# Strassen's scheme for 20 of the 28 F blocks of a GEGLU down projection, its sums made in place in shared memory

## The chip, the cores and the metric

The kernel runs on one core of a Trainium2 chip. The time is the device time of one execution in microseconds, median of several runs. The runs of the kernel before lie within 0.3% of each other. One early run of the kernel before took 1173.4 us, more than double the others. Being over 1.5% above the fastest it counts as slow and is left out. The traces show five engines that matter here: TensorE (PE, matmuls; PEld is its weight load), VectorE (DVE), ScalarE (ACT), GpSimd (POOL) and SyncE (SP), which issues most of the DMAs (108 of the 111 in the change's trace).

## The reference

```python
B, S, D, F = 1, 2048, 1024, 3584          # all bfloat16
def reference(x, w_gate, w_up, w_down):
    return (gelu_tanh(x @ w_gate) * (x @ w_up)) @ w_down
```

## The kernel before

The 2048 tokens are worked in two halves of 1024. Each half first makes h (gate and up, product with gelu) and keeps it in `hT`, 28 blocks of 128 F rows; then it computes down for two groups of 512 tokens. Gate and up already use Strassen's scheme (in Winograd's form): two F blocks and two halves of D make a 2 x 2 block product, which takes seven products and not eight. Its sums of weights (s1 to s4, on POOL) and of x (t1 to t4, on DVE, t4 on POOL) are fp32r tiles (fp32r is a 32-bit float type, printed as f32 in the rows of matmuls; one of 512 columns took 0.2286 us here, a bf16 one 0.2159); the plain blocks a22 and b22 are cast to fp32r by ACT. One `pair_quads` call makes two F blocks of gate and of up in 56 matmuls:

```python
for j in range(2):                                  # gate, up
    mm(PB[j], j, block(key, j, 0, 0), b11, True)    # m1, bf16
    act(nc.scalar.copy(out=banks[QB[j]][:], in_=banks[PB[j]][:]))
for j in range(2):
    mm(VB[j], j, s(j, "s1"), tsum["t1"], True)      # m5, fp32r
    ...
    prep(j, "s1")                                   # s1 of the next pair
# ... m6 = s2 t2 on QB, m2 on PB, m7 = s3 t3 on RB, m3 = s4 b22 on QB, m4 = a22 t4 on RB
```

Down is plain: per group 28 blocks x 8 banks of bf16 matmuls, `wd` streamed in tiles of two blocks, all eight of the kernel's `banks` in use.

```python
for kk, b in step:
    ts, dn = grp * TSB + b // 2, b % 2
    for c in range(WDT):
        nc.tensor.matmul(banks[b][:], lhsT=hT[:, kk * WDT + c, ts * P : (ts + 1) * P],
                         rhs=wd_tiles[base + kk][:, c, c0 : c0 + DN], ...)
```

In the down stage DVE, ACT and POOL have next to nothing to do but read the banks out and prepare the next half.

## Time and profile before

| | before |
|---|---|
| time, median of the fast runs | 562.3 us (562.25 to 562.6) |
| span of the profiled run | 560.4 us |
| PE busy | 552.3 us, 99% |
| one group of down (224 bf16 matmuls) | 48.35 us |
| one gate/up pair (16 bf16, 40 fp32r matmuls) | 12.60 us |
| granted clock of PE | 1.000 |

PE hardly waits in the two stages (0.9 us in front of all of down's matmuls, 1.4 in front of those of the pairs): the starts of its matmuls are evenly spaced (0.2159 us in down), so the time is the number of matmuls by their pace. The lines for that are in the prediction. Four more groups of the kernel before give the durations of what the change uses more of (line, engine, operation, out<-in, shapes, count | busy us, mean ns | idle before):

```profile
L340 PEld LDWEIGHTS bank<-t,s 128*128 128x128 f32 x624 | 117.4, 188 | 28.9
L444 PEld LDWEIGHTS <-hT 128*128 128x128 bf16 x896 | 87.5, 98 | 105.8 <-issue 0.5
L205 POOL TENSOR_TENSOR t<-xT,t 128x2048 fp32r<-128x2048 bf16 x2 | 8.2, 4081 | 0.0
L200 DVE TENSOR_TENSOR t<-xT,t 128x2048 fp32r<-128x2048 bf16 x2 | 4.6, 2287 | 9.7 <-DMA xT<-in_x_dram 9.7
```

The last two lines are how the change's sums look when nothing holds them up: DVE needs 2.3 us for 2048 columns, POOL 4.1.

### The profile page before, as it was taken

What the parts mean: (1) busy time and instruction counts of PE and PEld (TensorE: products, weight loads), DVE (VectorE), ACT (ScalarE), POOL (GpSimd) and SP (SyncE); (2) the same over time, 40 slices, a digit from 0 to 9 for tenths busy, and PEclk for the clock granted to TensorE, in tenths of its full rate; (3) what the DMA queues carried; (4) which work ended last, traced back from release to release, by engine and by line L of the source; (5) the groups of instructions that cost most, each with busy time, mean ns of one, the idle gap of its engine ahead of it and who ended that gap; (6) DMA issues with size and microseconds to landing.
All of it is one profiled execution on the core that took longest, in us unless ns stands there. A gap on an engine that the chain in (4) does not pass through costs nothing.

```text
span 560.4 us, 6719 instructions
## 1 busy us (share of the span) xinstructions
PE 552.3 (99%) x2475; PEld 334.9 (60%) x2521; DVE 175.7 (31%) x241; ACT 200.2 (36%) x342; POOL 248.2 (44%) x216
## 2 busy tenths in 40 slices
PE   8999999999999999999999999999999999999997
PEld 4457777667767544444467667767777664444443
DVE  1724444443344200113044443344444440001001
ACT  2435455555555100102055555555555540001001
POOL 0587777766774000003547766777777700000000
PEclk9999999999999999999999999999999999999999
DMA  9540412406100267987723140404070004446443
GB/s 274 176 149 2 150 61 91 131 20 205 58 2 1 60 192 226 254 236 240 256 77 95 56 150 2 150 1 150 22 241 3 0 1 135 158 155 230 151 150 112
DMA packets 61008, 67.54 MB, mean 121 GB/s; under 512 B 14768, under 2 KB 44720, under 8 KB 60976
## 3 DMA queue, kind: packets, MB, share of 16 engines
q1 hardware_dynamic: 60288, 66.46, 37.5%
q10 hardware_dynamic: 688, 0.66, 0.4%
q8 instruction: 20, 0.33, 0.2%
q14 instruction: 12, 0.10, 0.1%
HBM read 59.77 MB, written 4.19 MB: 114 GB/s over the span
## 4 chain that ended last, share of the span: by engine, by line
PE 98%; DMA 1%; issue 0%; ACT 0%; ACTq 0%
PE bank L340 58%; PE bank L444 34%; PE bank L211 5%; DMA wu_sb<-in_w_up_dram 1%; PE bank L265 0%; ACT o_sb L458 0%; ACTq L135 0%; ACTq L458 0%
## 5 line engine op out<-in xcount | busy, mean ns | idle before, releaser
L444 PE MATMUL bank<-wd_sb,hT 128*128 128x512 bf16 x878 | 192.8, 379 | 0.9
L340 PE MATMUL bank<-t,s 128*128 128x512 f32 x624 | 160.9, 406 | 0.0
L444 PEld LDWEIGHTS <-hT 128*128 128x128 bf16 x896 | 87.5, 98 | 105.8 <-issue 0.5
L316 POOL TENSOR_TENSOR s<-wg_sb 128x512 fp32r<-128x512 bf16 x52 | 62.2, 1196 | 198.8 <-DMA wg_sb<-in_w_gate_dram 105.3
L340 PEld LDWEIGHTS bank<-t,s 128*128 128x128 f32 x624 | 117.4, 188 | 28.9
L358 DVE TENSOR_TENSOR bank<-bank,m 128x512 f32<-128x512 f32 x104 | 72.6, 699 | 124.0 <-ACT bank L377 112.3
L226 DVE TENSOR_TENSOR hT<-g_sb,bank 128x512 bf16<-128x512 f32 x112 | 76.9, 688 | 68.0 <-ACT g_sb L221 31.1
L221 ACT ACTIVATE g_sb<-bank 128x512 f32<-128x512 f32 x112 | 66.6, 597 | 87.4 <-DVE bank L358 49.9
L458 ACT CAST o_sb<-bank 128x512 bf16<-128x512 f32 x16 | 9.4, 586 | 157.6 <-PE bank L444 140.3
L316 POOL TENSOR_TENSOR s<-wu_sb 128x512 fp32r<-128x512 bf16 x52 | 62.4, 1200 | 0.1
L460 DVE CAST o_sb<-bank 128x512 bf16<-128x512 f32 x16 | 11.1, 691 | 159.6 <-PE bank L444 136.4
L340 PE MATMUL bank<-xT,wg_sb 128*128 128x512 bf16 x183 | 52.5, 382 | 1.3
L340 PE MATMUL bank<-xT,wu_sb 128*128 128x512 bf16 x208 | 53.4, 379 | 0.1
L340 PE MATMUL bank<-b,s 128*128 128x512 f32 x208 | 51.4, 389 | 0.0
L340 PE MATMUL bank<-t,a 128*128 128x512 f32 x208 | 51.4, 389 | 0.0
L340 PEld LDWEIGHTS bank<-b,s 128*128 128x128 f32 x208 | 39.0, 188 | 8.2
L340 PEld LDWEIGHTS bank<-t,a 128*128 128x128 f32 x208 | 39.0, 188 | 8.1
L373 ACT COPY m<-bank 128x512 f32<-128x512 f32 x52 | 30.6, 588 | 17.7 <-PE bank L340 17.7
L377 ACT COPY bank<-bank 128x512 f32<-128x512 f32 x52 | 29.6, 570 | 17.0 <-PE bank L340 17.0
L329 ACT CAST a<-wg_sb 128x512 fp32r<-128x512 bf16 x26 | 16.2, 621 | 54.0 <-PE bank L340 29.2
L340 PEld LDWEIGHTS <-wu_sb 128*128 128x128 bf16 x208 | 20.3, 98 | 24.7 <-issue 0.3
L369 ACT COPY bank<-bank 128x512 f32<-128x512 f32 x52 | 29.6, 570 | 14.4 <-PE bank L340 13.6
(28 smaller groups left out, 238.2 us busy)
## 6 DMA issues: line engine op xcount, KB each, us to landing
wd_sb<-in_w_down_dram SPq DMA_DIRECT2D x56, 512.0 KB, 3.5
wg_sb<-in_w_gate_dram SPq DMA_DIRECT2D x11, 1024.0 KB, 5.4
wu_sb<-in_w_up_dram SPq DMA_DIRECT2D x11, 1024.0 KB, 7.5
out_dram<-o_sb SPq DMA_DIRECT2D x15, 256.0 KB, 2.7
wg_sb<-in_w_gate_dram SPq DMA_DIRECT2D x11, 256.0 KB, 4.0
wu_sb<-in_w_up_dram SPq DMA_DIRECT2D x11, 256.0 KB, 4.1
xs<-in_x_dram SPq DMA_DIRECT2D x2, 512.0 KB, 5.7
xT<-in_x_dram SPq DMA_TRANSPOSE x17, 3.8
```

The lines of the kernel that those rows point to most:

```text
L211: return nc.tensor.matmul(ps[:], lhsT=w_sb[:, kd, fi * P : (fi + 1) * P], rhs=xT[:, kd, tb * TB : (tb + 1) * TB], start=(kd == 0), stop=(k ...
L221: act(nc.scalar.activation(out=g_sb[:], in_=ps[:], func=ACT.Gelu_apprx_tanh))
L226: nc.vector.tensor_tensor(out=hT[:, fc, tb * TB : (tb + 1) * TB], in0=g_sb[:], in1=ps[:], op=ALU.mult,)
L316: pool(nc.gpsimd.tensor_tensor(out=t[:], in0=in0, in1=in1, op=op))
L329: act(nc.scalar.copy(out=t[:], in_=a(1, 1)))
L340: nc.tensor.matmul(banks[bank][:], lhsT=lhs[:, c, :], rhs=rhs[:, c, :], start=start and c == 0, stop=c == KH - 1, skip_group_check=True,)
L358: nc.vector.tensor_tensor(out=banks[dst][:], in0=banks[src][:], in1=m5[j][:], op=ALU.add)
L369: act(nc.scalar.copy(out=banks[QB[j]][:], in_=banks[PB[j]][:]))
L373: act(nc.scalar.copy(out=m5[j][:], in_=banks[VB[j]][:]))
L377: act(nc.scalar.copy(out=banks[RB[j]][:], in_=banks[QB[j]][:]))
L444: nc.tensor.matmul(banks[b][:], lhsT=hT[:, kk * WDT + c, ts * P : (ts + 1) * P], rhs=wd_tiles[base + kk][:, c, c0 : c0 + DN], start=(kk == ...
L460: dve(nc.vector.tensor_copy(out=dst, in_=banks[b][:]))
```

## The change

In down, the first 20 F blocks (as 2 x 10) against the two halves of D, and the first 256 against the last 256 tokens of a group, become a 2 x 2 block product by Strassen; the last 8 F blocks stay plain and add to the same banks. A group then needs 204 matmuls, of which 100 are fp32r, in place of 224 bf16 ones. The new sums get no memory of their own: they live in the memory of gate and up's sums (`t_mem`, `s_mem`), and the rows of `wd` in that of gate and up's weights (`w_mem`). Each sum overwrites the one before it: t2 replaces t1 block by block as m5 is done with it, t4 replaces t2, b22 replaces t3, and so for s. They are made anew for each of the four groups. The core of the diff:

```diff
+    t_mem = shared_pool.tile([P, 5 * KH * TB], F32R, name="t_mem")
+    s_mem = shared_pool.tile([P, 10 * KH * P], F32R, name="s_mem")
+    w_mem = shared_pool.tile([P, 4 * KD * FG + 4 * KD * P], BF16, name="w_mem")
 ...
+        product("m1", PB, h_block(0, 0), wd_block(0, 0), True)
+        # copy PB to QB (ACT)
+        product("m5", VB, lsum(0), rsum(0), True, behind=to_s2_t2)   # t2[i] DVE, s2[i] POOL
+        # copy VB to m5 (ACT)
+        product("m6", QB, lsum(0), rsum(0),
+            behind=lambda i: s_down(hT, grp, "s4", i, i + 1))        # POOL
+        for u in range(2):
+            act(nc.scalar.copy(out=banks[RB[u]][:], in_=banks[QB[u]][:]))
+            add_m5(QB[u], QB[u], u)                                  # DVE
+        for i in range(NS):
+            t_down("t4", i, i + 1)                                   # DVE
+        product("m2", PB, h_block(0, 1), wd_block(1, 0))
+        product("m7", RB, lsum(1), rsum(1), behind=lambda i: t_down("b22", i, i + 1))
+        for u in range(2):
+            add_m5(VB[u], RB[u], u)                                  # DVE: VB = RB + m5
+        # a22 (ACT)
+        product("m3", QB, lsum(0), rsum(1))
+        product("m4", RB, lsum(1), rsum(0))
+        # then 64 plain matmuls for the last 8 blocks, and the read-out
 ...
+        then0 = {                                # first group of a half
+            "m5": next_t("t3", 5),               # t3 of this group, DVE
+            "m4": next_t("t3", 5) + next_t("t1", 5) + [next_group],
+        }                                        # next_group: s1, s3 of the second group, POOL
```

(Cuts: comments in place of the copies, the loads, the sums' bodies and the last pair's `then`, in which s1, s3 and t1 of the first group are made.)

## The prediction

> **What bounds the kernel now.** I read the page's busy shares and slices, then the chain that ended last, then the timeline of TensorE (PE).
>
> ```profile
> PE 552.3 (99%) x2475; PEld 334.9 (60%) x2521; DVE 175.7 (31%) x241; ACT 200.2 (36%) x342; POOL 248.2 (44%) x216
> ...
> PEclk9999999999999999999999999999999999999999
> ...
> PE 98%; DMA 1%; issue 0%; ACT 0%; ACTq 0%
> PE bank L340 58%; PE bank L444 34%; PE bank L211 5%; DMA wu_sb<-in_w_up_dram 1%; PE bank L265 0%; ACT o_sb L458 0%; ACTq L135 0%; ACTq L458 0%
> ```
>
> PE is busy throughout at full clock, and is 98% of the chain; 34% is L444, the down matmuls. Busy is not pace, so I take paces from starts in PE's timeline:
>
> ```profile
> 161.79 1.04 PE L340 MATMUL bank<-xT,wg_sb 128*128 128x512 bf16 x3
> ...
> 174.39 1.04 PE L340 MATMUL bank<-xT,wg_sb 128*128 128x512 bf16 x3
> ...
> 186.99 96.87 PE L444 MATMUL bank<-wd_sb,hT 128*128 128x512 bf16 x439
> 283.69 0.81 PE L340 MATMUL bank<-xT,wg_sb 128*128 128x512 bf16 x3
> ```
>
> The down stage of one half is 283.69 - 186.99 = 96.70 us for 448 matmuls in the code (records are missing, x439): 0.2159 us each, 48.35 us per group of 224. A Strassen pair is 174.39 - 161.79 = 12.60 us for 16 bf16 and 40 fp32r matmuls, so an fp32r one costs (12.60 - 16 x 0.2159) / 40 = 0.2286 us. Only PE's work counts today. The other engines matter for what the change gives them, and one pair of rows warns about that, the first sums, where VectorE (DVE) and GpSimd (POOL) run together (timeline, 19.9 to 26.5 us):
>
> ```profile
> 20.02 2.28 DVE L200 TENSOR_TENSOR t<-xT,t 128x2048 fp32r<-128x2048 bf16 x1
> ...
> 20.64 2.68 POOL L316 TENSOR_TENSOR s<-wg_sb 128x512 fp32r<-128x512 bf16 x1 [19.33 <-DMA wg_sb<-in_w_gate_dram]
> ...
> 22.82 2.65 DVE L202 TENSOR_TENSOR t<-xT 128x2048 fp32r<-128x2048 bf16 x1
> ...
> 23.43 3.05 POOL L316 TENSOR_TENSOR s<-wu_sb 128x512 fp32r<-128x512 bf16 x1
> ...
> 26.44 1.15 POOL L316 TENSOR_TENSOR s<-s,wg_sb 128x512 fp32r<-128x512 f32 x1
> ```
>
> Alone, the POOL op takes 1.15 us. Here each ends about 1.01 us after the DVE sum beside it (22.30 to 23.32, 25.47 to 26.48), and the second DVE sum, 0.36 us longer than the first, ends 2.15 us after POOL's (23.32 to 25.47). They took turns.
>
> [...]a DVE op with one PSUM input doesn't stretch POOL (1.15 to 1.19 us within the pairs)[...]. [...]188 ns per fp32 load, 98 per bf16 load; at 0.2286 us per matmul the load is mostly hidden. [...]
>
> **Part by part, PE.** Per group, 20 F blocks go from 160 bf16 matmuls to 140: m1 and m2, 40 bf16; m5, m6, m7, m3, m4, 100 fp32r. The 8 plain blocks stay 64. New group: 104 x 0.2159 + 100 x 0.2286 = 22.45 + 22.86 = 45.31 us. That saves 3.04 us per group, 12.2 us over four groups: 562.3 - 12.2 = 550.1, 2.2% faster, if nothing waits.
>
> **Sums.** Each group needs t1 to t4 on DVE, 10 x 512 columns each, both inputs in SBUF; s1 to s4 on POOL, 10 x 256 columns each; b22 and a22 on ACT (about 10 x 0.62 and 5 x 0.62 us, behind m7 and m3, with some 2 us to spare). Taking turns, I estimate 0.55 us for 512 columns on DVE (2.15 / 4, rounded up) and 0.52 us for 256 on POOL (1.01 / 2, rounded up): a turn of both is 1.07 us. Alone they repeat every 0.60 and 0.63 us. All eight sums are 4 x 5.5 + 4 x 5.2 = 43 us of the shared way in per group, against 45 us of PE work. So it hardly has slack, and each sum has a deadline.
>
> **Second group of a half.** T is us from its m1. PE alone: m1 to 4.3, m5 to 8.9, m6 to 13.5, m2 to 17.8, m7 to 22.4, m3 to 26.9, m4 to 31.5, plain to 45.3. t2 and s2 are made in place, block by block, behind m5's reads, from T = 5.0; ten turns end at 15.7. m6 wants block 9 at 13.0; it ends at 16.3, so 2.8 us of wait. Then s4 has POOL nearly alone, t4 is done by about 27 and m4 may start at 29.7 as PE gets there. The group takes 45.3 + 2.8 = 48.1 us, 0.25 less than before.
>
> **First group of a half.** It starts behind, and has t3 to make as well. In the last gate/up pair t1 and the 1024-column pieces of s1 and s3 (2.0 us each) take turns, and DVE's order places t1 after the pair's adds; I get the last piece of t1 at T = 9.6, where m5's block 8 wants it at 8.0 (wait 1.6). POOL has done s2[0], s2[1]; eight turns to 18.2, two more t2 (with s4[0..1]) to 20.3; m6 ends at 20.8, 7.3 late in all. DVE then has, in order, t3 (5.4 us, three s4 between: 27.3), two adds of m5 (1.4: 28.7), three turns of t4 with s4 (31.9), seven t4 alone (36.1), and only then the adds of m5 to VB from RB (36.8, 37.5). m4 writes RB, so its second matmul waits to 37.5; PE would be there at about 34.5. m4 ends at 41.9, the plain blocks at 55.7. That is 7.3 us more than the old 48.35. Sums for the second group run in the plain part: t3, t1, s1 end near 53.5, s3 later; the next m5 is at 60, no wait.
>
> **Sum.** Two halves: 2 x (7.3 - 0.25) = 14.1 us more: about 576 us. As my turns may be pessimistic, and such a schedule was probably laid out with care, I put the point a little lower, at 574.
>
> **DMA.** wd falls from 56 loads of 0.5 MB to 16 plus 2 x 5 MB. The risk is the second group of the first half: two new weight chunks (2 MB each) and one wd tile stand ahead of the next wd tile in SP's queue. At 0.35 to 0.38 MB/us, as the DMA rate at 83 to 86 us shows, 4.7 MB from T = 27 land by about 42, the tile by 43.5, and PE wants it at about 45. Close, but I count nothing.
>
> **Rivals.** (1) Everything hides: 550 us. For it: PE never waits now, and the sums are cut so finely that PE could follow them. Against: the two stretched POOL rows. If only m6's short wait were left in each group, 4 x 2.8 gives 561. (2) The sums take turns as above and m6 and the first groups' m4 wait: 570 to 581; for it, the rows shown. (3) fp32r is slower here, as weights change bank at every matmul: each 0.01 us on 400 matmuls is 4 us; against, 40 in a row at 0.2286 now. (4) The wd tile late behind the chunks: 1 to 4 us, once. (5) PE's clock drops in the waits; the trace shows 0.9 or more in every slice, but has no such waits. It would add several us.
>
> **Range and chances.** 574 us, range 560 to 584: the low end is m6's wait alone, the high end rival 2 plus a few us of 3, 4 or 5. Faster by over 2% needs under 551.1, so no wait above 1 us in total: 0.06. Slower by over 2% needs over 573.6, near the middle of rival 2: 0.52. Within 2%: 0.42.
>
> **What would show it.** In the changed profile: first groups of about 55 us and second ones of about 48; PE waiting on POOL and DVE sums in m6 and on a DVE add at m4; POOL's 256-column sums stretched from about 0.65 to over 1 us and DVE's from 0.69 to over 1 where both run, and not where one runs alone; fp32r pace near 0.2286 where PE doesn't wait. The prediction is wrong if the small sums overlap unstretched, if a first group is under 50 us, or if the lost time is in front of a DMA.

The sum is 562.3 + 2 x (7.3 - 0.25) = 576.4 us, from which the point was set at 574. Its "0.60 and 0.63 us" are estimates that can be worked out from the trace of the kernel before: DVE starts its next operation 0.60 us after a 512-column one (22.22 to 22.82), and POOL's 512-column sums start 1.12 us apart (26.44 to 27.56), less 256 columns at 1.90 ns, (4081 - 1155) / 1536, for 0.63.

## The result, and the profile after

The change takes 590.7 us (590.0 to 590.9, 4 runs) against 562.3 us for the kernel before, ratio 1.050 (95% interval 1.048 to 1.052): slower. Ratios here are the mean time of one kernel's fast runs over that of the other's of the same rounds, so not quite the ratio of the medians that I quote.

The page after, for the lines shown of before:

```profile
PE 556.5 (95%) x2400; PEld 364.3 (62%) x2441; DVE 334.8 (57%) x365; ACT 244.5 (42%) x426; POOL 409.6 (70%) x328
PE   8999999999999795999999999999999997599897
DVE  0724443344446999778544434444434499994841
PEclk9999999999999997999999999999999999979999
PE 86%; DVE 8%; issue 3%; POOL 1%; DMA 1%; ACT 0%; DVEq 0%; POOLq 0%
```

PE's row has two dents (a 7 and a 5 close together, in each half's down stage), just where DVE's row goes to 9; the clock's row has a 7 at the 5 of the first half and next to that of the second; and DVE is now 8% of the chain that ended last. PE's busy time hardly moved though it has 75 records fewer: the dents cost what the matmuls saved, and more.

PE's timeline in the first half's down stage (start us, us, instructions, and the idle time before them with its releaser) shows the steps; the first group runs from 188.12 to 250.01:

```profile
188.12 4.49 PE L533 MATMUL bank<-w_mem,hT 128*128 128x512 bf16 x19
...
195.76 1.21 PE L533 MATMUL bank<-t_mem,s_mem 128*128 128x512 f32 x4 [0.39 <-DVE t_mem L491]
...
207.18 0.70 PE L533 MATMUL bank<-t_mem,s_mem 128*128 128x512 f32 x2 [0.38 <-DVE t_mem L491]
209.03 4.26 PE L533 MATMUL bank<-w_mem,hT 128*128 128x512 bf16 x19
212.94 9.44 PE L533 MATMUL bank<-t_mem,s_mem 128*128 128x512 f32 x40
228.85 7.49 PE L533 MATMUL bank<-t_mem,s_mem 128*128 128x512 f32 x20 [6.47 <-DVE bank L573]
236.18 13.99 PE L533 MATMUL bank<-wd_sb,hT 128*128 128x512 bf16 x62
250.01 4.48 PE L533 MATMUL bank<-w_mem,hT 128*128 128x512 bf16 x20
...
298.36 1.89 PE L361 MATMUL bank<-xT,w_mem 128*128 128x512 bf16 x8
```

The rows read as m1; m5 in pieces; m6 in pairs of matmuls every 1.08 us; m2; m7 and m3; then a gap of 6.47 us; m4, which takes 236.18 - 228.85 = 7.33 us where m7 and m3 took about 4.6 each; and the plain blocks. The group is 61.89 us long, against 48.35 before. The second group runs from 250.01 to 298.36, 48.35 us. The second half repeats it: 61.94 us for its first group. So the loss is 2 x 13.6 = 27.1 us in the first groups, and nothing in the second ones. The remaining 1.1 us of the profiled run is in its first 12 us, where PE was slow for longer: its first 16 small matmuls of x take 1.89 us and in the profile before 1.07 (the recorded clock is 1.00 in both, so it doesn't show why). In the profiles of e1 to e7, whose PE work is the same up to there, the first group starts at 186.95 to 188.61 us, so I don't charge this to the change.

What DVE and POOL did meanwhile, from their timelines:

```profile
193.23 11.09 POOL L510 TENSOR_TENSOR s_mem<-s_mem,hT 128x256 fp32r<-128x256 f32 x10 [0.86 <-PE bank L533]
204.28 14.24 POOL L510 TENSOR_TENSOR s_mem<-hT,s_mem 128x256 fp32r<-128x256 bf16 x10
218.90 7.43 POOL L510 TENSOR_TENSOR s_mem<-hT 128x512 fp32r<-128x512 bf16 x5 [0.38 <-PE bank L533]
...
197.24 10.87 DVE L491 TENSOR_TENSOR t_mem<-w_mem,t_mem 128x512 fp32r<-128x512 bf16 x10
208.03 7.05 DVE L491 TENSOR_TENSOR t_mem<-w_mem 128x1024 fp32r<-128x1024 bf16 x3
215.00 1.28 DVE L573 TENSOR_TENSOR bank<-bank,m 128x512 f32<-128x512 f32 x2
216.20 11.89 DVE L491 TENSOR_TENSOR t_mem<-w_mem,t_mem 128x512 fp32r<-128x512 bf16 x10
228.01 1.28 DVE L573 TENSOR_TENSOR bank<-bank,m 128x512 f32<-128x512 f32 x2
```

POOL's three rows are s2, s4 and the next group's s1; DVE's are t2, t3, the adds to QB, t4 and the adds to VB. t2 takes 1.08 us a block beside s2. t4 takes 11.89 us, about 1.6 us a block in the stretch beside s1, although t4 and s1 share no data. DVE is busy without a break from 197 to 229 us, and the last thing in its queue is what m4 waits for: m4 writes RB, and the adds to VB read RB.

The clock, by stretches (window, its length, busy us and count of PE, PEld, DVE, ACT, POOL; then PE's granted clock, DMA share, GB/s):

```profile
222.40:228.85 6.45, 0.00 (x1) 0.03 (x1) 6.45 (x7) 0.00 (x0) 3.94 (x3) 0.91 0.00 0
228.85:232.00 3.15, 3.15 (x7) 2.40 (x8) 3.15 (x3) 0.00 (x0) 0.85 (x1) 0.50 0.00 0
232.00:236.20 4.20, 4.20 (x15) 3.11 (x14) 4.20 (x3) 0.00 (x0) 4.20 (x2) 0.71 0.00 0
```

During the gap the granted clock fell to half (0.50 from 227.64 to 234.48 us, worked out from windows of 1 us), and m4 then ran through 5.6 us of it.

### The profile page after: what moved, and what is told of

It is laid out like the page before. It is cut to its first block, busy times and chain, and to the rows that moved or that the text cites. A ratio compares the mean times of both kernels' runs of the same rounds, so it can differ in the third digit from the quotient of the medians.

```text
span 588.5 us, 7109 instructions
## 1 busy us (share of the span) xinstructions
PE 556.5 (95%) x2400; PEld 364.3 (62%) x2441; DVE 334.8 (57%) x365; ACT 244.5 (42%) x426; POOL 409.6 (70%) x328
## 4 chain that ended last, share of the span: by engine, by line
PE 86%; DVE 8%; issue 3%; POOL 1%; DMA 1%; ACT 0%; DVEq 0%; POOLq 0%
PE bank L361 54%; PE bank L533 27%; DVE t_mem L491 8%; PE bank L229 5%; POOL s_mem L510 1%; DMA w_mem<-in_x_dram 1%; PE bank L283 0%; DVE hT L244 0%; DVE bank L384 0%; DVE bank L573 0%; ACT o_sb L643 0%; DVEq L491 0%; DVEq L244 0%; POOLq L510 0%
## 5 line engine op out<-in xcount | busy, mean ns | idle before, releaser
L361 PE MATMUL bank<-t_mem,s_mem 128*128 128x512 f32 x1040 | 255.2, 399 | 0.0
L361 PEld LDWEIGHTS bank<-t_mem,s_mem 128*128 128x128 f32 x1040 | 195.4, 188 | 45.3
L335 POOL TENSOR_TENSOR s_mem<-w_mem 128x512 fp32r<-128x512 bf16 x104 | 121.6, 1190 | 111.1 <-PE bank L361 81.2
L533 PE MATMUL bank<-t_mem,s_mem 128*128 128x512 f32 x400 | 108.5, 418 | 24.9 <-DVE bank L573 12.9
L533 PEld LDWEIGHTS bank<-t_mem,s_mem 128*128 128x128 f32 x400 | 75.9, 197 | 55.2 <-POOL s_mem L510 22.0
L361 PE MATMUL bank<-xT,w_mem 128*128 128x512 bf16 x392 | 97.7, 380 | 1.3
L491 DVE TENSOR_TENSOR t_mem<-w_mem,t_mem 128x512 fp32r<-128x512 bf16 x80 | 84.3, 1123 | 8.2 <-PE bank L533 8.2
L510 POOL TENSOR_TENSOR s_mem<-hT 128x512 fp32r<-128x512 bf16 (+1 forms) x32 | 67.7, 2142 | 18.8 <-PE bank L533 10.4
L491 DVE TENSOR_TENSOR t_mem<-w_mem 128x1024 fp32r<-128x1024 bf16 (+2 forms) x28 | 64.5, 2352 | 0.0
L335 POOL TENSOR_TENSOR s_mem<-s_mem,w_mem 128x512 fp32r<-128x512 f32 x52 | 63.3, 1240 | 0.0
L335 POOL TENSOR_TENSOR s_mem<-w_mem,s_mem 128x512 fp32r<-128x512 bf16 x52 | 60.0, 1175 | 0.0
L533 PE MATMUL bank<-wd_sb,hT 128*128 128x512 bf16 x248 | 55.4, 379 | 0.4
```

The costliest lines, as they stand in the source:

```text
L335: pool(nc.gpsimd.tensor_tensor(out=t, in0=in0, in1=in1, op=op))
L361: nc.tensor.matmul(banks[bank][:], lhsT=lhs[:, c, :], rhs=rhs[:, c, :], start=start and c == 0, stop=c == KH - 1, skip_group_check=True,)
L491: dve(nc.vector.tensor_tensor(out=t, in0=in0, in1=in1, op=ALU.subtract))
L510: pool(nc.gpsimd.tensor_tensor(out=t, in0=in0, in1=in1, op=op))
L533: nc.tensor.matmul(banks[bank][:], lhsT=lhs, rhs=rhs, start=start, stop=stop, skip_group_check=True,)
```

## The experiments

The theory after reading the trace: (a) a DVE sum with two SBUF inputs and a POOL sum exclude each other; (b) in the first groups that makes DVE's queue the bound, with s1 of the next group in it as an uninvited guest, as nothing in its data holds it behind t4; (c) m4 hangs on DVE's order, not on its own data; (d) the gap costs a second time, through the clock. The rivals: the small sums are slow by themselves; fp32r matmuls are slower in down; m4 is slow because of its operands. Each run below is beside the kernel before on the same chip (medians 563.6, 562.2 and 562.4 us for the three sets). "First" and "second" are the groups of a half; two numbers are those of both halves. The group times are those of the profiled run, which for e5_split is its slowest (589.65 us, where the fastest took 586.45).

| run | time us | ratio (95%) | first groups us | second group us, first half |
|---|---|---|---|---|
| before | 562.3 | 1 | 48.35 | 48.35 |
| the change | 590.7 | 1.050 (1.048 to 1.052) | 61.9, 61.9 | 48.4 |
| e3_write (wrong result) | 551.2 | one look | 45.3, 45.3 | 45.2 |
| e1_hold | 576.7 | 1.023 (1.021 to 1.026) | 56.3, 54.7 | 48.4 |
| e2_fill | 587.1 | 1.042 (1.040 to 1.044) | 59.5, 61.1 | 48.3 |
| e4_add | 585.9 | 1.040 (1.038 to 1.041) | 59.2, 60.0 | 49.5 |
| e5_split | 587.6 | 1.045 (1.042 to 1.048) | 62.1, 62.2 | 48.0 |
| e6_holdadd | 573.7 | 1.020 (1.018 to 1.021) | 52.5, 52.5 | 50.9 |
| e7_dve24 | 570.2 | 1.013 (1.011 to 1.015) | 53.2, 53.2 | 46.9 |
| e8_dve | 571.5 | 1.018 (1.014 to 1.021) | 49.1, 49.1 | 55.3 |
| e10_chunk | 558.2 | 0.993 (0.991 to 0.994) | 49.1, 49.1 | 45.4 |
| e11_s3 | 557.3 | 0.991 (0.989 to 0.992) | 48.0, 48.0 | 45.6 |

All but e3_write gave the reference's result.

### Do the sums exclude each other? (e3_write)

```diff
-        pool(nc.gpsimd.tensor_tensor(out=t, in0=in0, in1=in1, op=op))
+        for _ in range(2):
+            pool(nc.gpsimd.memset(t.bitcast(F32), 0.5))
```

> Wrong result on purpose: every down sum on GpSimd becomes two memsets of the same block, which write SBUF and read nothing. Theory, the clash is at the reads of SBUF: DVE's 512-column sums fall from 1.08 and 1.65 us apart to 0.60 even where GpSimd is busy, m6 and m4 don't wait, groups of 45.3 to 46, time about 550 to 553. Rival, any work on GpSimd slows DVE, or DVE is slow in place: DVE's spacing stays above 0.8 us where GpSimd is busy and m6 still waits.

DVE's and POOL's timelines, first group:

```profile
193.19 6.11 DVE L491 TENSOR_TENSOR t_mem<-w_mem,t_mem 128x512 fp32r<-128x512 bf16 x10
205.96 6.10 DVE L491 TENSOR_TENSOR t_mem<-w_mem,t_mem 128x512 fp32r<-128x512 bf16 x10
...
193.21 12.53 POOL L511 MEMSET s_mem<- 128x256 f32 x40 [2.75 <-PE bank L534]
```

POOL is busy without a break beside t2 (40 memsets in 12.53 us), but it no longer reads SBUF, and t2 takes 6.11 us for ten blocks and not 10.87. That clears the small sums on DVE and leaves the exclusion at the reads. The time of this single run was 551.2 us and the groups 45.25 us: the prediction's 45.31 us of PE work for a group, so fp32r is not slower in down either. This is what the change is worth when its sums are free.

### The guest in the queue (e1_hold)

```diff
+        def hold_pool():      # one column of t4's last block: waits for t4
+            pool(nc.gpsimd.tensor_copy(out=hold_sb[:],
+                in_=right(0, NS - 1, NS)[:, 0, DN - 1 :].bitcast(F32)))
-            "m4": next_t("t3", 5) + next_t("t1", 5) + [next_group],
+            "m4": [hold_pool] + next_t("t3", 5) + next_t("t1", 5) + [next_group],
```

> The next group's s1 sums are held on GpSimd until t4 is done (a one-column copy that reads t4's last block). Theory, DVE and GpSimd take turns at SBUF and s1 ran ahead into t4: t4 drops from 11.9 to about 7.5 us, PE's wait before m4 from 6.45 to about 2 us, m4 then stays at full clock (4.6 us and not 7.3), each first group falls from 61.9 to about 55, the time to about 577. Rival, DVE's small sums are slow by themselves: t4 stays near 11.9 us, time 590. Second groups stay at 48.35 in both.

t4 in the first half, PE's m4 in both, and the clock in the first half:

```profile
216.70 7.06 DVE L491 TENSOR_TENSOR t_mem<-w_mem,t_mem 128x512 fp32r<-128x512 bf16 x10
...
224.52 6.72 PE L534 MATMUL bank<-t_mem,s_mem 128*128 128x512 f32 x20 [1.62 <-DVE bank L574]
505.57 5.11 PE L534 MATMUL bank<-t_mem,s_mem 128*128 128x512 f32 x20 [1.65 <-DVE bank L574]
...
226.00:228.00 2.00, 2.00 (x6) 1.59 (x5) 2.00 (x2) 0.00 (x0) 2.00 (x2) 0.50 0.00 0
```

t4 took 7.06 us as expected and the gap 1.62 us: 14.0 us of the time came back. That shows theory (b). One thing was not as expected: the clock halved here too, after a much shorter gap. In the second half the gap was as long (1.65 us), the clock stayed at 1.00 and m4 took 4.96 us; the two first groups differ by that, 56.3 and 54.7 us. The four runs show the same two outcomes: two have a mean granted clock of 0.997 (578.3 and 578.0 us), two of 1.000 (575.3 us both).

### Is it the gap that makes m4 slow? (e2_fill)

```diff
+        if grp == 0:
+            for i in range(20):                      # adds zero to m2's banks
+                mm(PB[i % 2], zero_sb[:], b_block(0, 0, 0, 1)[:, 0, :])
         product("m4", RB, lsum(1), rsum(0))
```

> 20 matmuls by a zero weight, added to m2's bank, fill 4.3 us of PE's wait before m4 in the first groups. Theory, m4 ran at half clock because PE sat idle for 6.45 us: the granted clock stays 1.0 in m4, it takes 4.5 to 4.7 and not 7.3 us, time about 585 (2 x 2.8 less). Rival, m4 is slow because its operands or banks come late, one by one: m4 stays 7.3 us, time 590 to 591.

In the first half m4 took 4.95 us at clock 1.00, in the second half 6.55 us with the clock at half for part of it, though the rest of the gap was the same in both (2.13 and 2.12 us). The time fell by 3.6 us of the 5.7 expected. So the theory holds where the clock held, m4's operands are cleared, and after a gap of 2 us the clock can go either way. A fill that leaves less of a gap was not tried.

### Does m4 need t4 or DVE's order? (e4_add, then e6_holdadd)

```diff
-        for i in range(NS):
+        for i in range(5):
             t_down("t4", i, i + 1)
 ...
             add_m5(VB[u], RB[u], u)
+        for i in range(5, NS):
+            t_down("t4", i, i + 1)
```

> The two adds of m5 to VB from RB move ahead of the last five t4 blocks in DVE's order. Theory, m4 waits for all of t4 only by DVE's order (it writes RB, which those adds read): m4 starts right behind m3 and then follows t4 block by block, ending some 4 us earlier in each first group, clock at full or nearly, time about 582. Rival, m4 waits for the t4 data itself: its last block sets the end either way, at best 1 to 2 us less per group, time 587 or more. In second groups nothing changes.

m4 did start right behind m3 (0.60 us of gap), so the wait was one of order. But t4's last five blocks still took turns with s1 at about 1.6 us each, PE followed them two matmuls at a time, and the clock halved in that sparse stretch (no gap over 0.92 us, PE busy 55% and 35% of the two 2 us windows from 226 to 230 us; 0.50 from 231.2 to 233). The gain was 4.8 us and not 9: the rival was nearer on the size, as the order and s1 cover for each other. The second group of the first half, 49.5 us, waited 1.00 us for a late `wd` tile; more on that below. Both edits together tell that:

> Both earlier edits of the first groups: s1 of the next group held until t4 is done, and the adds of m5 to VB ahead of t4's last five blocks. Theory, these were two separate causes of one wait, and the half clock its sequel: first groups fall from 56.3 (hold alone) to about 53, m4 at 4.6 us and full clock, time about 570. Rival, the hold took the whole wait already and the rest is in m5 and m6: time 574 to 577.

The first groups fell to 52.5 us, under the 53 expected, and the clock stayed up (1.00 in both groups of the first half). The time did not reach 570, as the second group of the first half lost 2.5 us: its m6 waited longer, as s3, now later, ran on into it (the hold's one-column copy itself took 8.32 us here, beside DVE's sums of t3 and t1, and 0.18 in e1_hold), and a `wd` tile came 1.52 us late. This is the transfer that the prediction had called close: two weight chunks for the next half stand ahead of it in SP's queue. What made it late is the edit itself: the `w_up` part of the first chunk goes where t4 reads rows of `wd`, t4's last blocks now come after m7's adds, and SP sends the first piece of `w_up` 28.8 us after the group's start and not 25.6 as in the change (28.0 in e4_add). e1_hold, with shorter first groups but t4 in its old place, sends it at 25.6 and has no late tile.

### Is m6's wait the sums' pace? (e5_split)

The first half of m2 moves ahead of m6:

```diff
+        product("m2", PB, h_block(0, 1), wd_block(1, 0), i1=5)
         product("m6", ...)
 ...
-        product("m2", PB, h_block(0, 1), wd_block(1, 0))
+        product("m2", PB, h_block(0, 1), wd_block(1, 0), i0=5)
```

> The first half of m2 (10 bf16 matmuls, 2.16 us, no sums needed) moves between m5 and m6. Theory, PE waits in m6 for ten turns of t2 and s2, and in the first groups m4's start is set by DVE's queue, not by PE: second groups fall from 48.35 to about 46.2 us, first groups stay at 61 to 62, time about 586.5. Rival, fp32r matmuls are slower in the down stage and the loss lies there: second groups stay near 48.3, time 590.

The second group went to 48.0 us, of which 0.93 us was the late `wd` tile: 47.1 us where 46.2 was expected and 48.35 was the rival. m6 ended 16.6 us after the group's start, as in the change (16.8), though 2.16 us of other work had been put ahead of it: PE's work was hidden in the wait, and t2 and s2 set its end. The first groups stayed at 62 us, as expected. So fp32r's pace is out as a cause, but most of this move's gain was taken back at once by the tile and by small waits behind it; alone it is worth 0.5% at best.

### Sums that exclude each other, on the faster engine (e7_dve24, e8_dve)

```diff
-        pool(nc.gpsimd.tensor_tensor(out=t, in0=in0, in1=in1, op=op))
+        if name in DVE_S or (name, grp) in DVE_S:
+            dve(nc.vector.tensor_tensor(out=t, in0=in0, in1=in1, op=op))
+        else:
+            pool(nc.gpsimd.tensor_tensor(out=t, in0=in0, in1=in1, op=op))
+    DVE_S = ("s2", "s4")        # e7; its hold, as in e1_hold, is cut here
```

> With the hold, s2 and s4 are made on DVE, not on GpSimd (0.33 us for 256 columns by 1.04 ns a column, where GpSimd takes 0.52 in its turn). Theory, sums that exclude each other cost least on the faster engine: t2 and s2 together 0.93 us a block and not 1.08, second groups about 46.9, first ones about 52.5, time about 566. Rival, two engines still overlap in part and one engine with more work is slower: m6 ends later than now, time above 577.

```profile
241.45 4.48 PE L539 MATMUL bank<-w_mem,hT 128*128 128x512 bf16 x20
256.76 4.26 PE L539 MATMUL bank<-w_mem,hT 128*128 128x512 bf16 x19
...
288.31 1.89 PE L361 MATMUL bank<-xT,w_mem 128*128 128x512 bf16 x8
```

The second group is 288.31 - 241.45 = 46.86 us, the 46.9 expected: a block of t2 and s2 now takes 0.94 us on one engine, and took 1.08 us on two; on DVE a 256-column sum gives way to the next operation after 0.33 us (196.98 to 197.31). The 1.04 ns a column is an estimate from the kernel before, (2287 - 688) / 1536 for DVE's operations of 2048 and 512 columns. The first groups are 53.2 us (52.5 expected), the time 570.2 (566 expected). The rival is out.

e8_dve goes on: all down sums on DVE but the first s1, t1 earlier in the last pair, m2 split, the adds to QB ahead of s4, the adds to VB ahead of t4.

> All of it: every down sum on DVE but the first s1 (GpSimd, in the last pair, while DVE reads PSUM), t1 started earlier in that pair, m2 split around m6, adds to QB ahead of s4 and to VB ahead of t4. Theory, the change's arithmetic is worth having once the sums don't exclude each other: second groups 45.3 to 45.6 us (no wait), first groups 48 to 50, time about 559, just under the kernel before. Rival, the sums are too many for DVE's order in the first groups: these stay above 52, time above 565.

The first groups came to 49.1 us in both halves, as expected. The second ones did not, for two new waits that the trace names:

```profile
239.94 5.95 PE L538 MATMUL bank<-w_mem,hT 128*128 128x512 bf16 x19 [2.92 <-DVE o_sb L655]
286.80 5.30 PE L538 MATMUL bank<-wd_sb,hT 128*128 128x512 bf16 x15 [3.46 <-DMA wd_sb<-in_w_down_dram]
...
521.07 4.26 PE L538 MATMUL bank<-w_mem,hT 128*128 128x512 bf16 x19 [2.92 <-DVE o_sb L655]
```

m1 of the second group waited for DVE to read the banks out behind the sums in its queue, and the `wd` tile came 3.46 us late (t4 is last in DVE's order here, and SP's first piece of `w_up` went out 32.6 us after the group's start). Both gaps of the first half brought the half clock with them (0.53 on average from 240 to 243 us, 0.83 from 286 to 289): m1 took 5.95 us for what takes 4.3. In the second half a gap as long, 2.92 us, did not slow it: m1 took 4.26 us.

### A version that is faster than both (e10_chunk, e11_s3)

Both start from e8_dve. The cut shows what e10_chunk adds to it (the call of the new `done("end")` is left out); e11_s3 also makes 4 blocks of the first groups' s3 on POOL.

```diff
-                on_act = b % 2 == (1 if last_grp else 0)
+                on_act = grp == 0 or b % 2 == (1 if last_grp else 0)
 ...
-                lambda: w_fill(1),                  # after the group's first plain step
+            then1["end"] = [lambda: w_fill(1)]      # after its last wd tile
```

> The version of before with every down sum on DVE, and its two leftovers mended: the first groups' banks are read out by ACT alone (m1 of the second group had waited 2.92 us for DVE's read-out behind the sums), and the second weight chunk of the next half is loaded after the group's last wd tile (a tile had come 3.46 us late behind it). Theory: these waits and the half clocks after them go, first groups 49, second 45.3 to 46, time 558 to 560, just faster than the kernel before (ratio 0.992 to 0.996). Rival, ACT's read-outs or the chunk then come late: time above 563.

> As the run beside it, and 4 of the 10 blocks of the first groups' s3 are made on GpSimd in the last pair, where DVE mostly reads PSUM. Theory: 1.1 us less in DVE's queue ahead of t3, so m7 waits about 1 us less in each first group, 48 us each, time about 557. Rival, GpSimd's pieces hold up t1 on DVE and m5 waits instead: no gain, 559 or more.

Both came in as expected, 558.2 and 557.3 us. e11_s3 is 0.9% faster than the kernel before (ratio 0.991, 0.989 to 0.992): clear of the noise. Its page and PE's timeline:

```profile
PE 547.1 (98%) x2400; PEld 360.9 (65%) x2441; DVE 319.9 (58%) x463; ACT 247.7 (45%) x434; POOL 265.2 (48%) x226
...
188.37 4.49 PE L538 MATMUL bank<-w_mem,hT 128*128 128x512 bf16 x19
236.39 4.48 PE L538 MATMUL bank<-w_mem,hT 128*128 128x512 bf16 x20
281.96 1.89 PE L361 MATMUL bank<-xT,w_mem 128*128 128x512 bf16 x8
```

The second group is 45.57 us, 0.3 above PE's work alone; the first is 48.02, so 2.7 us of DVE's queue is still on the path there. The late tile is down to a wait of 0.21 us. DVE has less busy time than in the change (320 us against 335) with more work, as its records are no longer stretched beside POOL's: its 512-column sums t2 and t4 last 0.685 us on average and not 1.123.

## Why the prediction was wrong

It said slower, at 574 us with 584 as its upper end; 590.7 lies above. Point by point:

- **PE's work** was right: 45.31 us a group, 45.25 measured where nothing waits (e3_write).
- **The turns** were right: 1.07 us a block said, 1.08 measured; the second groups 48.1 said, 48.35 measured; m6 in the first group ending at T = 20.8, measured 209.03 - 188.12 = 20.9. Rival 2 was the right one for m6; its range, 570 to 581, was missed all the same, for the next point.
- **The step that failed is the end of the first group**: "seven t4 alone (36.1), and only then the adds of m5 to VB from RB (36.8, 37.5)" and "m4 ends at 41.9". Two terms of it were mis-sized. First, t4 was not alone: the prediction placed the next group's sums "in the plain part", where the program text has them, but POOL began s1 as soon as m3 had read the first blocks of s4 (218.90 us, T = 30.8). t4 took 11.89 us where three turns and seven alone are 7.4; as it began 0.6 us earlier than said, m4 started 3.9 us late, at T = 40.7 and not at 36.8. With s1 held, t4 took 7.06 us and the time was 576.7 us, within the range (e1_hold). Second, m4 was given 5.1 us (36.8 to 41.9, with its second matmul's wait) and took 7.33, as PE's clock halved in the gap. The prediction had this as rival 5 and left it out of the timetable; e2_fill showed m4 at 4.95 us where the clock held. Together 3.9 + 2.2 = 6.1 us per first group: 55.7 said, 61.9 measured. Twice 6.2 us is 12.4 of the 14.3 us between the timetable's 576.4 and the result; the start of the run (1.1 us in the profile) and the second groups (twice 0.25) are most of the rest.
- **Lowering the point from 576 to 574** because "my turns may be pessimistic" had no ground in the trace, and went the wrong way.
- **The DMA** was rightly not counted for the change itself, where no wait of that kind shows. It was as close as said, though the recorded sum has a slip (4.7 MB from T = 27 at 0.35 MB/us land by 40.4, not 42): in e5_split, where SP issues the tile at the same T as in the change (38.1 and 38.2), it landed at T = 44.6, and the change wants it at 44.9. The kernels that moved t4's last blocks back met it (e4_add 1.00, e6_holdadd 1.52, e8_dve 3.46 us), and e5_split (0.93), whose plain part begins 1.4 us earlier; e1_hold, e2_fill and e7_dve24 did not, although their first groups are shorter than the change's.

What stays open: how much idle time PE's clock bears. The same 1.6 us gap halved it in one half and not in the other (e1_hold), and so with 2.1 us (e2_fill) and 2.9 us (e8_dve). The stretches at half clock were 3.4 us long in the first half of e1_hold, the second half of e2_fill and the first half of e4_add, and 6.84 us in both halves of the change (227.64 to 234.48 and 514.36 to 521.20 us); these are estimates from the mean clock of windows of 1 to 3 us, which is 1.00 or 0.50 in the windows wholly outside or inside a stretch. What decides whether a gap brings one was not shown by any run.

## What to carry to other kernels

Before giving two engines a share of the same stage, check in the trace whether their operations stretch each other (in the change DVE's 512-column sums last 1.16 us beside s2 and 1.65 beside s1, against 0.68 alone); if they take turns, put the work on the engine that is faster per column (here DVE with 1.04 ns against POOL's 1.90, both estimated above from the kernel before), and count one queue, not two. Here an instruction ran when its own engine's order and its data allowed, not where the program text has it (s1 at 218.90 us, 10 us before m4), so ask of every off-path operation what really holds it back. A gap in PE's work can cost more than its length, through the clock: here gaps of 1.62, 2.12 and 2.92 us did, and others of 1.65, 2.13 and 2.92 us did not.
